# The first loads of q and k cut at another head, fewer filler matmuls, and the last token tile finished in two column halves

## The chip, the cores and the metric

The kernel runs on one core of a Trainium2 chip. The core has five instruction streams: TensorE (PE, matrix products; PEld is its weight load), VectorE (DVE), ScalarE (ACT), GpSimd (POOL) and SyncE (SP, which here only starts transfers). Each stream runs its instructions in program order and waits on semaphores for what the others and the DMA transfers deliver. The metric is the device time of one execution in microseconds (us); lower is better.

## The reference, cut to what matters

Three stages follow one another, all in fp32, on 2 x 576 = 1152 tokens and 512 features (8 heads of 64):

```python
# 1 attention with a causal window of 128 and a bias by distance
scores = q @ k.T / 8;  scores = where(mask, scores - slope_h * |rel|, -1e9)
x = softmax(scores) @ v                       # (B=2, H=8, S=576, D=64) -> (1152, 512)
# 2 dense mixture of 4 experts, F = 1024
p = probs / probs.sum(-1);  x = sum_e p[:, e] * (relu(x @ w1[e]) @ w2[e])
# 3 squared-relu MLP, F = 2048
h = relu(x @ w_in);  out = (h * h) @ w_out
```

## The kernel before

**The work.** fp32 products are made from two rounded parts of each operand (names ending in h and l), so a product is three matmuls. The exception is the very start, where the first 128 tokens of both batch rows are taken in plain fp32 ("raw"): q and k as they were loaded, without a split. The attention is cut into units. A unit of the start covers one pair of heads, 2c and 2c+1 (c = 0 to 3), of both batch rows b, over the first 128 tokens; the text calls these units c0 to c3. For each, `scores` (L802) does four matmuls, g = 0 to 3, with batch row g // 2 and head 2c + g % 2; `top` (L821) reads them on DVE (bias, row minimum); `exp` (L834) runs on ACT; `inv` and `norm` (L842, L850) divide; `turn` (L864) transposes on PE; `hi` (L881) copies; `pv` (L713) multiplies by v. Score tiles have two PSUM buffers (`sc=2`), so the scores of c2 wait until DVE has read those of c0.

**What sets the order.** The class `Plan` (L37) orders the start and the attention at build time: every task has estimated durations on the engines that may run it, dependencies, buffers and a due time, and the planner emits instructions in the order of its own estimated clock. On the chip each engine then follows this fixed order. Where the planner expects PE to stand idle before a task that calls `keep_busy` (L519), it emits small bf16 matmuls of a zero tile (`idle`, 128x128) into the PSUM tile that the task will overwrite; the text calls them fillers. Their number is (expected gap + lead) / each. `plan.at["PE"]` has already been moved past the task when `keep_busy` reads it, so the branch `early` never applies before: lead is -0.2 and each is 0.08 everywhere.

**The first loads.** `first_load` (L1406) brings the first 128 columns of q and k for all 8 heads, 1 MB in all: eight transfers of four heads and one batch row, 128 KB each, into 64 partitions, 512 B per row. Half 0 (heads 0 to 3) serves c0 and c1, half 1 (heads 4 to 7) serves c2 and c3. k of half 0 is started by ACT, the rest by SP, then v and the first weights by SP. In the planner's estimate, c0 and c1 depend on the two tasks of half 0.

```python
src[b, 4 * half:4 * half + 4, 0:D, 0:P]               # L1414, one transfer
lhsT=first_in["q", c // 2][0:D, g // 2, 2 * (c % 2) + g % 2, :]   # L809
```

**The end.** The MLP's last quarters of F run in pairs of token chunks (`gemm1_pair` L1052, `gemm2_pair` L1136). `flush_one` (L1274) does the second product for quarter f of a chunk: for the last chunk (5 token tiles of 128) the quarters f = 2 and f = 3 are summed in one PSUM bank per tile, six matmuls of 512 columns per tile and quarter. After quarter 3 `evac` (L1182) adds the bank to the running sum `ytile` on DVE and SP starts the store to DRAM (L1207). Tile 7 (the fourth of the five) crosses two segments of tokens and is stored by two transfers of 64 rows; tile 8, the last, by one of 128 rows.

Of the kernel before, what the change touches and what calls it, by code (L numbers as in the profile page):

```python
# [8 lines left out]
F32 = mybir.dt.float32  # L9
# [4 lines left out]
ALU = mybir.AluOpType  # L14
PSUM = bass.MemoryType.PSUM

P = 128
# [8 lines left out]
PAIRS = [(0, 256), (512, 320)]  # L26
# [104 lines left out]
def kernel(  # L131
# [14 lines left out]
    nc = tc.nc  # L146
    B, H, _, S = qT.shape
    D = v.shape[2] // H
    NT, DM = out.shape
    E, _, F = w1.shape  # L150
# [5 lines left out]
    NQ = 4  # L156
# [26 lines left out]
    NE = len(w1s)  # L183
# [22 lines left out]
    def w_tile(shape, dtype, name):  # L206
        i = free.pop(0)
        return wbuf[i].tile(shape, dtype, tag=f"wb{i}", name=name), i
# [110 lines left out]
    def spent(eng, us, lag=0.0):  # L319
        clock[eng] = max(clock[eng], clock["now"] + lag) + us  # L320
        return clock[eng]
# [133 lines left out]
    def overlap(a0, an, b0, bn):  # L455
        a, b = max(a0, b0), min(a0 + an, b0 + bn)
        return (a, b - a) if a < b else None

    def tile_runs(nt):

        col = 0
        for s0, sn in SEGS:
            hit = overlap(col, sn, nt * P, P)
            if hit:
                yield hit[0] - nt * P, s0 + hit[0] - col, hit[1]
            col += sn

    def chunks(e):
        return CHUNKS if e else CHUNKS0
# [5 lines left out]
    plan = Plan(SLOTS)  # L475
# [4 lines left out]
        sc=[actx.enter_context(tc.tile_pool(name="psc", bufs=2, space=PSUM))],  # L480
# [4 lines left out]
    def ps_tile(kind, shape, name):  # L485
        pool = psum[kind][0]
        psum[kind].append(psum[kind].pop(0))
        return pool.tile(shape, F32, tag=kind, name=name)
# [30 lines left out]
    def keep_busy(place):  # L519


        early = plan.at["PE"] < 1.0 and plan.gap > 2.0
        lead, each = (0.6, 0.11) if early else (-0.2, 0.08)
        for _ in range(int(max(plan.gap + lead, 0.0) / each)):
            nc.tensor.matmul(  # L525
                out=place, lhsT=idle, rhs=idle, start=True, stop=True, skip_group_check=True
            )
# [45 lines left out]
    def tile_n(t):  # L573
        return min(P, S - t * P)
# [209 lines left out]
    def job_tasks(u, i, t, add, b_, end, ready, G, q0, k0, pos, wide):  # L784
        c = units[u]["c"]
        n = tile_n(t)
# [4 lines left out]
        s = {k: Buf(k) for k in ("sc", "ts", "st", "tp")}  # L791
        cols = [(0, n)] if t == 0 else [(0, P), (P, n)]
        rows = [cn for _, cn in cols]
        key = "j%d" % i
        last = state.get("last", {})
# [6 lines left out]
        def scores(eng):  # L802
            sc = s["sc"].tile = ps_tile("sc", [P, G, w], "sc")
            keep_busy(sc[:, 0, 0:P])
            qs = slice(t * P - q0, t * P - q0 + n)
            for g in range(G):
                if raw:
                    nc.tensor.matmul(
                        out=sc[0:n, g, :], lhsT=first_in["q", c // 2][0:D, g // 2, 2 * (c % 2) + g % 2, :],  # L809
                        rhs=first_in["k", c // 2][0:D, g // 2, 2 * (c % 2) + g % 2, :],  # L810
                        start=True, stop=True,
                    )
                    continue
                for ql in (b_["qh"].tile, b_["ql"].tile):
                    nc.tensor.matmul(  # L815
                        out=sc[0:n, g, :], lhsT=ql[:, g, qs],
                        rhs=b_["khl"].tile[:, g, j0:j0 + w],
                        start=(ql is b_["qh"].tile), stop=(ql is b_["ql"].tile),
                    )
# [120 lines left out]
    ytile = {}  # L940
# [192 lines left out]
        fill(0.6, step, 0.8 + 1.4 * (2 * n // P))  # L1133
        return h

    def gemm2_pair(e, ch, g, h, tile_, first, last):  # L1136
        (wh, _), (wl, _) = w2t[e, g]
        i, y = tile_
        ns = slice(i * P, (i + 1) * P)
        for fo, (hh, hl) in enumerate(h):  # L1140
            for j, (l_, r_) in enumerate(((hh, wh), (hh, wl), (hl, wh))):
                nc.tensor.matmul(  # L1142
                    out=y, lhsT=l_[:, ns], rhs=r_[:, fo, :],
                    start=(first and fo == 0 and j == 0),
                    stop=(last and fo == FTQ - 1 and j == 2),
                )
# [35 lines left out]
    def evac(e, ch, tiles, f=0, two=False):  # L1182
        c0 = PAIRS[ch][0] if two else chunks(e)[ch][0]
        for i, y in tiles:
            nt = c0 // P + i
            if e == 0 or (e == E and f < FT // 2):
                pool = yp if nt < 4 else late["w"]
                ytile[nt] = pool.tile([P, DM], F32, tag=f"y{nt}", name="y")
            yt = ytile[nt]
            spent("ACT" if e == E and f < FT // 2 else "DVE", 0.74, 1.38 if two else 0.69)  # L1190
            if e == 0:
                nc.vector.tensor_scalar(
                    out=yt, in0=y, scalar1=pt[:, nt, 0:1], scalar2=None, op0=ALU.mult
                )
            elif e < E:
                nc.vector.scalar_tensor_tensor(
                    out=yt, in0=y, scalar=pt[:, nt, e:e + 1], in1=yt, op0=ALU.mult, op1=ALU.add
                )
            elif e == E and f < FT // 2:
                nc.scalar.activation(out=yt, in_=y, func=ACTF.Copy)  # L1200
            elif e == E:
                nc.vector.tensor_tensor(out=yt, in0=y, in1=yt, op=ALU.add)
            else:
                nc.vector.tensor_tensor(out=yt, in0=y, in1=yt, op=ALU.add)
            if e == NE - 1 and f == NQ - 1:
                for r0, n0, n in tile_runs(nt):
                    nc.sync.dma_start(out=out[n0:n0 + n, :], in_=yt[r0:r0 + n, :])  # L1207

    def to_x2(nt, kind):
        tp = ps_tile(kind, [P, KT, P], "xtp")  # L1210
        for k in range(KT):
            nc.tensor.transpose(  # L1212
                out=tp[:, k, :], in_=ytile[nt][:, k * P:(k + 1) * P], identity=ident
            )
        ns = slice(nt * P, (nt + 1) * P)
        spent("ACT", 0.6)
        spent("DVE", 0.7)
        nc.scalar.activation(out=xh[:, :, ns], in_=tp, func=ACTF.Copy)
        nc.vector.tensor_tensor(out=xl[:, :, ns], in0=tp, in1=f32(xh[:, :, ns]), op=ALU.subtract)
# [46 lines left out]
    ys = {}  # L1266
# [7 lines left out]
    def flush_one():  # L1274
        e, ch, f, h, two = pend.pop(0)
        if two:
            first, last = f % 2 == 0, f % 2 == 1
        else:
            n = FT // 2 if e == E else FT
            first, last = f % n == 0, f % n == n - 1  # L1280
        if first:
            n = 2 * PAIRS[ch][1] if two else chunks(e)[ch][1]
            ys[e, ch] = [(i, ps_tile("y", [P, DM], "yacc")) for i in range(n // P)]
        for tile_ in ys[e, ch]:
            if two:
                gemm2_pair(e, ch, f, h, tile_, first, last)
            else:
                gemm2(e, ch, f, h, [tile_], first, last)
            if last:
                evac(e, ch, [tile_], f, two)  # L1290
            elif two:
                run_x2("work")
            i = len(ys[e, ch]) - 1 - tile_[0]
            need = 0.8 + (1.38 - 0.74 * last) * i if two else 3.0 + 0.69 * i
            fill(0.5 if two and last else 1.0, 1.38 if two else 0.69, need)
        w_done(w2t, e, ch, f, two)
        if last:
            tiles = ys.pop((e, ch))
            if e == E - 1 and f == NQ - 1:
                x2todo.extend(PAIRS[ch][0] // P + i for i, _ in tiles)  # L1300
# [96 lines left out]
    for c in range(NP):  # L1397
        for own in (True, False):
            task["bias", c, own] = plan.add(
                "bias", [("DVE", 0.45, 0.5), ("ACT", 0.5, 0.6)],  # L1400
                lambda eng, c=c, own=own: build_bias(c, own, eng), deps=[t_rel],
                due=(8.0 if own else 20.0) + c,
            )
    first_in, first_buf, first_x, first_h = {}, [], [], {}

    def first_load(what, half):  # L1406
        t, buf = w_tile([P, 2, 4, P], F32, "first")
        first_buf.append(buf)
        first_in[what, half] = t
        src = qT if what == "q" else kT  # L1410
        queue = nc.scalar if (what, half) == ("k", 0) else nc.sync
        for b in range(B):
            queue.dma_start(
                out=t[0:D, b], in_=src[b, 4 * half:4 * half + 4, 0:D, 0:P].rearrange("a p s -> p a s")  # L1414
            )

    def first_v():
# [5 lines left out]
    for half in range(2):  # L1423
        for i, what in enumerate("qk"):
            task["first", what, half] = plan.add(
                "first" + what, [("ACT" if (what, half) == ("k", 0) else "SP", 1.3, 5.2 if half else 4.2)],
                lambda eng, what=what, half=half: first_load(what, half), due=half + 0.1 * i,
# [235 lines left out]
    for i in range(PER):  # L1663
        weight_load(i)
    t_pt = plan.add("pt", [("SP", 0.6, 6.0)], lambda eng: nc.sync.dma_start(
        out=pt, in_=probs.rearrange("(t p) e -> p t e", p=P)
# [41 lines left out]
    for it, (e, ch, f, two) in list(enumerate(items))[N1:]:  # L1708
# [4 lines left out]
        g = f if two else f // FTQ  # L1713
# [6 lines left out]
        if two:  # L1720
# [4 lines left out]
            h = gemm1_pair(e, ch, f)  # L1725
        else:
# [4 lines left out]
            h = gemm1(e, ch, f)  # L1731
# [22 lines left out]
        last = not two and (e, ch, f) in ((0, len(CHUNKS0) - 1, FT - 1), (E, len(CHUNKS) - 1, FT - 1))  # L1754
# [37 lines left out]
```

## Time and profile before

| | us |
|---|---|
| median of 3 runs | 665.21 (665.19 to 665.52) |
| profiled execution | 664.39 |
| its span (first to last instruction) | 662.6 |
| PE busy | 654.7 |
| DVE, POOL, ACT busy | 471.2, 386.3, 315.2 |

The profiled execution's own time is 1.8 us longer than its span. Engine columns count execution of instructions, not waits; L numbers are lines of the kernel above. "PE busy" is by modelled ends of pipelined matmuls, and the fillers count as busy, too.

### The profile page before, as it was taken

The numbers are of one execution on the slowest core, as the hardware profiler recorded it, in microseconds if no ns is written. First come the engines' busy times: TensorE is split into PE (matmuls) and PEld (weight loads), VectorE is DVE, ScalarE is ACT, GpSimd is POOL, SyncE is SP. The second block draws the span as 40 slices with busy tenths as digits, with TensorE's granted clock in tenths as the row PEclk, the third lists the DMA queues.
The fourth block names the chain that finished last, engine by engine and source line by source line (L and its number), as shares of the span: only waits on it lengthen the run. The fifth ranks groups of instructions, "written<-read, shape, count | busy, mean of one in ns | idle before, by whom it ended". The sixth has DMA issues, their size and how long they took to land.

```text
span 662.6 us, 10910 instructions
## 1 busy us (share of the span) xinstructions
PE 654.7 (99%) x3899; PEld 587.7 (89%) x3899; DVE 471.2 (71%) x989; ACT 315.2 (48%) x763; POOL 386.3 (58%) x457
## 2 busy tenths in 40 slices
PE   9999999999999999999999999999999999999997
PEld 8879988889898898989999899898999999898996
DVE  6998987748888777877876876776578654545453
ACT  6998877624444344343443434333465534334120
POOL 1799966528776653654565454421568984856331
PEclk9999999999999999999999999999999999999999
DMA  9952221021404334344244344344122001100012
GB/s 237 270 144 77 72 77 42 11 65 60 162 33 136 110 124 154 114 128 158 81 144 143 110 145 143 128 161 157 54 91 80 1 14 50 65 1 1 0 65 79
DMA packets 44022, 64.42 MB, mean 97 GB/s; under 512 B 4160, under 2 KB 26176, under 8 KB 43968
## 3 DMA queue, kind: packets, MB, share of 16 engines
q1 hardware_dynamic: 32704, 39.35, 19.3%
q10 hardware_dynamic: 11264, 24.38, 11.7%
q8 instruction: 30, 0.49, 0.3%
q14 instruction: 24, 0.20, 0.1%
HBM read 52.97 MB, written 10.75 MB: 96 GB/s over the span
## 4 chain that ended last, share of the span: by engine, by line
PE 91%; DVE 3%; ACT 2%; POOL 2%; issue 1%; DMA 1%; POOLq 0%; ACTq 0%
PE yacc L1142 30%; PE hps L1064 27%; PE hps L950 13%; PE yacc L1177 13%; PE xps L735 2%; PE tp L871 2%; PE sc L815 2%; PE hps L1589 1%; ACT ts L837 1%; PE sc L525 1%; POOL ts L859 1%; PE xtp L1212 1%; DVE fxwork L986 1%; DMA rk<-in_kT_dram 1%; POOL ql L501 0%
## 5 line engine op out<-in xcount | busy, mean ns | idle before, releaser
L1142 PE MATMUL yacc<-wh,hmem 128*128 128x512 f32 x576 | 183.7, 390 | 0.0
L501 POOL TENSOR_TENSOR wl<-wraw,wh 128x256 fp32r<-128x256 f32 (+1 forms) x107 | 102.9, 986 | 64.3 <-ACT wh L434 51.4
L1142 PEld LDWEIGHTS yacc<-wh,hmem 128*128 128x128 f32 x576 | 108.2, 188 | 21.8
L1142 PE MATMUL yacc<-wl,hmem 128*128 128x512 f32 x288 | 112.4, 390 | 0.0
L1177 PE MATMUL yacc<-wh,hmem 128*128 128x512 f32 x272 | 89.4, 393 | 0.0
L501 POOL TENSOR_TENSOR ls<-wsum,hs 128x256 fp32r<-128x256 f32 x64 | 54.5, 878 | 48.0 <-ACT hs L381 47.5
L1075 ACT ACTIVATE p<-hps 128x256 f32<-128x256 f32 (+1 forms) x64 | 26.3, 410 | 97.8 <-PE hps L1064 97.2
L950 PE MATMUL hps<-xh,wh 128*128 128x384 f32 (+1 forms) x208 | 66.6, 320 | 0.0
L950 PE MATMUL hps<-xh,wl 128*128 128x384 f32 (+1 forms) x208 | 65.5, 315 | 0.0
L950 PE MATMUL hps<-xl,wh 128*128 128x384 f32 (+1 forms) x208 | 65.4, 315 | 0.0
L1079 DVE TENSOR_TENSOR u<-hps,p 128x256 f32<-128x256 f32 (+1 forms) x64 | 29.1, 455 | 50.0 <-PE hps L1064 49.8
L1142 PEld LDWEIGHTS yacc<-wl,hmem 128*128 128x128 f32 x288 | 54.1, 188 | 10.1
L1177 PEld LDWEIGHTS yacc<-wh,hmem 128*128 128x128 f32 x272 | 51.1, 188 | 10.1
L292 DVE SCALAR_TENSOR_TENSOR wconv<-wraw,wconv 128x512 int32<-128x512 int32 x64 | 57.3, 895 | 1.3
L1099 ACT ACTIVATE hmem<-c 128x256 fp32r<-128x256 f32 (+1 forms) x72 | 31.0, 445 | 54.1 <-DVE c L1079 52.8
L501 POOL TENSOR_TENSOR la<-wraw,ha 128x256 fp32r<-128x256 f32 x48 | 44.5, 950 | 20.4 <-ACT ha L367 20.4
L1177 PE MATMUL yacc<-wl,hmem 128*128 128x512 f32 x136 | 53.2, 391 | 0.0
L501 POOL TENSOR_TENSOR hmem<-c,hmem 128x256 fp32r<-128x256 f32 (+1 forms) x32 | 26.9, 859 | 38.3 <-ACT hmem L1095 38.3
L501 POOL TENSOR_TENSOR hmem<-r,hmem 128x384 fp32r<-128x384 f32 x24 | 26.2, 1092 | 39.1 <-ACT hmem L1164 39.1
L1100 DVE SCALAR_TENSOR_TENSOR hmem<-c,hmem 128x256 fp32r<-128x256 f32 (+1 forms) x72 | 38.5, 555 | 14.6 <-ACT hmem L1099 13.3
L837 ACT ACTIVATE ts<-ts,st 128x256 f32<-128x256 f32 (+2 forms) x80 | 37.1, 466 | 7.1 <-DVE st L828 7.0
L950 PEld LDWEIGHTS hps<-xh,wh 128*128 128x128 f32 x208 | 39.2, 189 | 0.7
(142 smaller groups left out, 1738.2 us busy)
## 6 DMA issues: line engine op xcount, KB each, us to landing
wraw<-in_w_dram SPq DMA_DIRECT2D x32, 512.0 KB, 4.1
wraw<-in_w_out_dram ACTq DMA_DIRECT2D x16, 512.0 KB, 3.9
w<-wconv ACTq DMA_DIRECT2D x32, 256.0 KB, 3.9
wraw<-w SPq DMA_DIRECT2D x16, 512.0 KB, 3.7
wraw<-in_w_in_dram ACTq DMA_DIRECT2D x14, 512.0 KB, 3.7
rq<-in_qT_dram SPq DMA_DIRECT2D x8, 256.0 KB, 7.2
out_dram<-y SPq DMA_DIRECT2D x8, 256.0 KB, 2.1
rk<-in_kT_dram SPq DMA_DIRECT2D x8, 192.0 KB, 5.7
```

Source lines behind the costliest of these rows:

```text
L292: nc.vector.scalar_tensor_tensor(out=ai, in0=raw[j][:, :, part], scalar=amount, in1=ai, op0=op, op1=ALU.bitwise_or,)
L501: e.tensor_tensor(out=out, in0=in0, in1=f32(in1), op=ALU.subtract)
L735: nc.tensor.matmul(out=xps[:, :, o0:o0 + w], lhsT=l_, rhs=r_, start=(i == 0 and l_ is wh_ and r_ is hi), stop=(i == len(mm) - 1 and l_ is ...
L837: nc.scalar.activation(out=ts[0:n, g, :], in_=ts[0:n, g, :], func=ACTF.Exp, bias=st[0:n, 0, g:g + 1], scale=-1.0, accum_out=st[0:n, 1, g:g ...
L950: nc.tensor.matmul(out=ps, lhsT=l_[:, k, cs], rhs=r_[:, k, cols], start=(k == 0 and r_ is xh and l_ is wh and not second), stop=(k == KT - ...
L1064: nc.tensor.matmul(out=ps, lhsT=a[l_][:, k, :], rhs=b[r_][:, k, :], start=start and k == 0 and l_ == r_, stop=stop and k == 1 and l_ == 1, ...
L1075: nc.scalar.activation(out=out, in_=x, func=ACTF.Copy)
L1079: nc.vector.tensor_tensor(out=out, in0=x, in1=y, op=ALU.add)
L1099: nc.scalar.activation(out=hh, in_=src, func=ACTF.Relu)
L1100: nc.vector.scalar_tensor_tensor(out=hl, in0=src, scalar=0.0, in1=f32(hh), op0=ALU.max, op1=ALU.subtract)
L1142: nc.tensor.matmul(out=y, lhsT=l_[:, ns], rhs=r_[:, fo, :], start=(first and fo == 0 and j == 0), stop=(last and fo == FTQ - 1 and j == 2),)
L1177: nc.tensor.matmul(out=y, lhsT=l_[:, ns], rhs=r_[:, fo, :], start=(first and j == 0), stop=(last and j == 2),)
```

## The change

Three edits. `first_load` now cuts after head 1: for each of q, k and each batch row there is one transfer of heads 0 and 1 (64 KB) and one of heads 2 to 7 (192 KB); ACT starts three of them (both small ones of k, then the large one of k for b = 0), SP the other five. The planner's tasks and their estimates stay as they are. `keep_busy` subtracts 1.4 or 1.2 us in place of 0.2 from the expected gap, early in the plan. And the last token tile of the last chunk takes a new function `close`: its quarter 2 gets a bank of its own, which DVE adds to `ytile` at once, and its quarter 3 is made in two halves of 256 columns, each in its own bank, with its own add and its own store, the first half's store from SP, the second half's from ACT.

```diff
@@ keep_busy
-        early = plan.at["PE"] < 1.0 and plan.gap > 2.0
-        lead, each = (0.6, 0.11) if early else (-0.2, 0.08)
-        for _ in range(int(max(plan.gap + lead, 0.0) / each)):
+        lead = -1.4 if plan.at["PE"] < 6.0 else -1.2 if plan.at["PE"] < 9.0 else -0.2
+        for _ in range(int(max(plan.gap + lead, 0.0) / 0.08)):
@@ scores
-                        out=sc[0:n, g, :], lhsT=first_in["q", c // 2][0:D, g // 2, 2 * (c % 2) + g % 2, :],
-                        rhs=first_in["k", c // 2][0:D, g // 2, 2 * (c % 2) + g % 2, :],
+                        out=sc[0:n, g, :], lhsT=first_in["q", g // 2][0:D, 2 * c + g % 2, :],
+                        rhs=first_in["k", g // 2][0:D, 2 * c + g % 2, :],
@@ gemm2_pair
-                    out=y, lhsT=l_[:, ns], rhs=r_[:, fo, :],
+                    out=y, lhsT=l_[:, ns], rhs=r_[:, fo, cols],
@@ new
+    def close(e, ch, f, h, i):
+        nt = PAIRS[ch][0] // P + i
+        if f < NQ - 1:
+            y = ps_tile("y", [P, DM], "yacc")
+            gemm2_pair(e, ch, f, h, (i, y), True, True)
+            nc.vector.tensor_tensor(out=ytile[nt], in0=y, in1=ytile[nt], op=ALU.add)
+            return
+        for cs, queue in ((slice(0, DM // 2), nc.sync), (slice(DM // 2, DM), nc.scalar)):
+            y = ps_tile("work", [P, DM // 2], "ylast")
+            gemm2_pair(e, ch, f, h, (i, y), True, True, cs)
+            yt = ytile[nt][:, cs]
+            nc.vector.tensor_tensor(out=yt, in0=y, in1=yt, op=ALU.add)
+            for r0, n0, n in tile_runs(nt):
+                queue.dma_start(out=out[n0:n0 + n, cs], in_=yt[r0:r0 + n, :])
@@ flush_one
         for tile_ in ys[e, ch]:
+            if (e, ch) == (NE - 1, len(PAIRS) - 1) and f >= NQ - 2 and tile_ is ys[e, ch][-1]:
+                close(e, ch, f, h, tile_[0])
+                break
@@ first_load
-        for b in range(B):
+        some, most = slice(0, 2), slice(2, H)
+        for b, heads in {
+            ("q", 0): ((0, some), (1, some)), ("k", 0): ((0, some), (1, some), (0, most)),
+            ("q", 1): ((0, most), (1, most)), ("k", 1): ((1, most),),
+        }[what, half]:
+            queue = nc.scalar if (what, half) == ("k", 0) else nc.sync
             queue.dma_start(
-                out=t[0:D, b], in_=src[b, 4 * half:4 * half + 4, 0:D, 0:P].rearrange("a p s -> p a s")
+                out=first_in[what, b][0:D, heads, :],
+                in_=(qT if what == "q" else kT)[b, heads, 0:D, 0:P].rearrange("a p s -> p a s"),
```

By this the fillers before the scores of c0 fall from 51 to 36, those before the scores of c2 from 17 to 5; the later groups (20, 1 and 6) stay. No other instruction of the start changes its place in its stream.

PE at the start, before: the scores of c0 (tile sc_158) and of c1 (sc_214), after the 51 fillers. The DMAHW names are the semaphores of the eight first transfers.

```order
L808 MATMUL sc_158<-first_127,first_124 128x128 [waits DMAHW1_49,DMAHW0_49]
L808 MATMUL sc_158<-first_127,first_124 128x128
L808 MATMUL sc_158<-first_127,first_124 128x128 [waits DMAHW3_49,DMAHW2_49]
L808 MATMUL sc_158<-first_127,first_124 128x128
L808 MATMUL sc_214<-first_127,first_124 128x128 x4
```

The same place now, after 36 fillers: c0 is sc_158, c1 is sc_199.

```order
L807 MATMUL sc_158<-first_128,first_124 128x128 [waits DMAHW1_49,DMAHW0_49]
L807 MATMUL sc_158<-first_128,first_124 128x128
L807 MATMUL sc_158<-first_129,first_125 128x128 [waits DMAHW3_49,DMAHW2_49]
L807 MATMUL sc_158<-first_129,first_125 128x128
L807 MATMUL sc_199<-first_128,first_124 128x128 [waits DMAHW5_49,DMAHW4_49]
L807 MATMUL sc_199<-first_128,first_124 128x128
L807 MATMUL sc_199<-first_129,first_125 128x128 [waits DMAHW7_49,DMAHW6_49]
L807 MATMUL sc_199<-first_129,first_125 128x128
```

Before, c1 waits for no transfer that c0 has not waited for. Now c1 waits for the other four of the eight first transfers.

SP's first transfers before: q of half 0, q of half 1, k of half 1, then v and the first weights.

```order
L1413 DMA first_124<-in_qT_dram 64x4x128 x2
L1413 DMA first_130<-in_qT_dram 64x4x128 x2
L1413 DMA first_147<-in_kT_dram 64x4x128 x2
L1421 DMA first_156<-in_v_dram 128x2x512
L215 DMA wraw_224<-in_w1_dram 128x4x256
```

SP's first transfers now: heads 0 and 1 of q for both batch rows, heads 2 to 7 of q, heads 2 to 7 of k for b = 1, then v and the first weights.

```order
L1440 DMA first_124<-in_qT_dram 64x2x128
L1440 DMA first_125<-in_qT_dram 64x2x128
L1440 DMA first_124<-in_qT_dram 64x6x128
L1440 DMA first_125<-in_qT_dram 64x6x128
L1440 DMA first_129<-in_kT_dram 64x6x128
L1449 DMA first_156<-in_v_dram 128x2x512
L215 DMA wraw_209<-in_w1_dram 128x4x256
```

SP has one transfer fewer ahead of v (five, six before); ACT has one more ahead of its first computation (three, two before).

DVE at the very end, before: the five adds of the last chunk, tile 4 to tile 8 (y_5929).

```order
L1204 TENSOR_TENSOR y_5751<-yacc_7145,y_5751 128x512
L1204 TENSOR_TENSOR y_5759<-yacc_7146,y_5759 128x512
L1204 TENSOR_TENSOR y_5906<-yacc_7147,y_5906 128x512
L1204 TENSOR_TENSOR y_5915<-yacc_7148,y_5915 128x512
L1204 TENSOR_TENSOR y_5929<-yacc_7149,y_5929 128x512
```

The same place now; tile 8 is y_5902, its quarter 2 comes first.

```order
L1214 TENSOR_TENSOR y_5902<-yacc_7146,y_5902 128x512
L1203 TENSOR_TENSOR y_5724<-yacc_7118,y_5724 128x512
L1203 TENSOR_TENSOR y_5732<-yacc_7119,y_5732 128x512
L1203 TENSOR_TENSOR y_5879<-yacc_7120,y_5879 128x512
L1203 TENSOR_TENSOR y_5888<-yacc_7121,y_5888 128x512
L1220 TENSOR_TENSOR y_5902<-ylast_7187,y_5902 128x256
L1220 TENSOR_TENSOR y_5902<-ylast_7196,y_5902 128x256
```

DVE has one add of 512 columns more, and two of 256 columns in place of the last one. On PE, twelve matmuls of 256 columns end the program where six of 512 did.

## Rows read from the trace of the kernel before

**Rows 1.** The page: the chain that ended last, share of each engine.
```profile
PE 91%; DVE 3%; ACT 2%; POOL 2%; issue 1%; DMA 1%; POOLq 0%; ACTq 0%
```

**Rows 2.** Stretches: length, PE, PEld, DVE, ACT, POOL busy, granted clock, DMA share, GB/s.
```profile
0.00:20.00 20.00, 18.56 (x187) 16.25 (x187) 13.94 (x68) 14.70 (x53) 4.67 (x11) 1.00 0.97 237
40.00:50.00 10.00, 9.09 (x52) 6.61 (x51) 8.74 (x24) 9.26 (x27) 10.00 (x9) 1.00 0.54 149
```

**Rows 3.** Timeline of the start: start, length, engine, line, operation, count, idle before.
```profile
0.98 4.70 PE L525 MATMUL sc<-idle 128*128 128x128 bf16 x51 [0.98 <-DVE idle L1389]
0.98 3.92 PE L525 MATMUL sc<-idle 128*128 128x128 bf16 x37 [0.98 <-DVE idle L1389]
6.96 0.29 DVE L828 CUSTOM_DVE_ANT_0 ts<-sc,bias 128x128 f32<-128x128 f32 x1 [3.27 <-PE sc L808]
7.94 1.11 PE L525 MATMUL sc<-idle 128*128 128x128 bf16 x17
7.96 0.29 DVE L828 CUSTOM_DVE_ANT_0 ts<-sc,bias 128x128 f32<-128x128 f32 x1
9.38 0.69 DVE L853 TENSOR_TENSOR ts<-ts,st 128x512 f32<-128x512 f32 x1
10.18 0.29 DVE L828 CUSTOM_DVE_ANT_0 ts<-sc,bias 128x128 f32<-128x128 f32 x1
14.94 0.69 DVE L853 TENSOR_TENSOR ts<-ts,st 128x512 f32<-128x512 f32 x1
```

**Rows 4.** The chain that ended last, at the start: start, length, what.
```profile
5.68 1.25 PE sc L808 x8
9.05 1.10 PE sc L808 x8
10.51 3.20 ACT ts L837 x16
```

**Rows 5.** Timeline: issues of the second q transfer and the last k transfer.
```profile
1.56 0.83 SPq L1413 DMA_DIRECT2D first<-in_qT_dram  x1
4.46 0.62 SPq L1413 DMA_DIRECT2D first<-in_kT_dram  x1
```

**Rows 6.** Landing after issue (us, last number): first k, second q, last k transfer.
```profile
first<-in_kT_dram ACTq DMA_DIRECT2D x1, 128.0 KB, 3.0
first<-in_qT_dram SPq DMA_DIRECT2D x1, 128.0 KB, 4.5
first<-in_kT_dram SPq DMA_DIRECT2D x1, 128.0 KB, 4.5
```

**Rows 7.** Stretches (columns as rows 2): first loads on two queues, then on SP's alone.
```profile
3.00:4.50 1.50, 1.50 (x17) 1.50 (x16) 0.68 (x6) 1.49 (x7) 0.00 (x0) 1.00 0.97 211
4.75:7.25 2.50, 2.50 (x30) 2.31 (x28) 0.29 (x3) 0.01 (x1) 0.00 (x0) 1.00 1.23 183
```

**Rows 8.** Timeline of the end: last add, last two issues of stores.
```profile
658.50 0.69 DVE L1204 TENSOR_TENSOR y<-yacc,y 128x512 f32<-128x512 f32 x1 [0.67 <-PE yacc L1142]
658.42 0.59 SPq L1207 DMA_DIRECT2D out_dram<-y  x1
659.22 0.42 SPq L1207 DMA_DIRECT2D out_dram<-y  x1
```

**Rows 9.** The end: two stretches of the stores, and the last store's landing.
```profile
659.60:659.80 0.20, 0.00 (x0) 0.00 (x0) 0.00 (x0) 0.00 (x0) 0.00 (x0) 1.00 0.83 205
660.40:660.60 0.20, 0.00 (x0) 0.00 (x0) 0.00 (x0) 0.00 (x0) 0.00 (x0) 1.00 1.03 389
out_dram<-y SPq DMA_DIRECT2D x1, 256.0 KB, 2.3
```

**Rows 10.** Matmuls of 256 columns in a row; DVE adds of 256 columns (mean ns).
```profile
30.46 0.28 PE L950 MATMUL hps<-xl,wh 128*128 128x256 f32 x1
30.58 0.28 PE L950 MATMUL hps<-xh,wl 128*128 128x256 f32 x1
L1079 DVE TENSOR_TENSOR u<-hps,p 128x256 f32<-128x256 f32 x1 | 0.4, 425 | 1.7 <-PE hps L1064 1.7
```

More of the change, by code (lines that the diff above doesn't have):

```diff
@@ L1134, in gemm1_pair, with gemm2_pair @@
         return h
-    def gemm2_pair(e, ch, g, h, tile_, first, last):
+    def gemm2_pair(e, ch, g, h, tile_, first, last, cols=slice(0, DM)):
         (wh, _), (wl, _) = w2t[e, g]
@@ L1282, in flush_one @@
             n = 2 * PAIRS[ch][1] if two else chunks(e)[ch][1]
-            ys[e, ch] = [(i, ps_tile("y", [P, DM], "yacc")) for i in range(n // P)]
+            ending = (e, ch, f) == (NE - 1, len(PAIRS) - 1, NQ - 2)
+            ys[e, ch] = [
+                (i, None if ending and i == n // P - 1 else ps_tile("y", [P, DM], "yacc"))
+                for i in range(n // P)
+            ]
         for tile_ in ys[e, ch]:
+            if (e, ch) == (NE - 1, len(PAIRS) - 1) and f >= NQ - 2 and tile_ is ys[e, ch][-1]:
+                close(e, ch, f, h, tile_[0])
+                break
             if two:
@@ L1406, in first_load @@
     def first_load(what, half):
[L1407 to L1411, printed above, removed]
-        for b in range(B):
+        if half == 0:
+            for b in range(B):
+                t, buf = w_tile([P, H, P], F32, "first")
+                first_buf.append(buf)
+                first_in[what, b] = t
+        some, most = slice(0, 2), slice(2, H)
[4 more added lines that the diff above has]
+            queue = nc.scalar if (what, half) == ("k", 0) else nc.sync
             queue.dma_start(
-                out=t[0:D, b], in_=src[b, 4 * half:4 * half + 4, 0:D, 0:P].rearrange("a p s -> p a s")
+                out=first_in[what, b][0:D, heads, :],
+                in_=(qT if what == "q" else kT)[b, heads, 0:D, 0:P].rearrange("a p s -> p a s"),
             )
```

## The prediction, written before the changed kernel was run

> **What bounds the kernel now.** I read the page first, then stretches of time, then the timeline and the landing of single transfers in the two places that the change touches. The page's chain is PE for 91% [rows 1], so anything that holds PE back early is paid at the end unless a later wait swallows it. The stretches say how much could be swallowed: PE stands idle for 1.44 us of the first 20, and for 0.91 us between 40 and 50, where POOL is busy 10.00 of 10 [rows 2].
>
> The start is a relay of three engines. PE runs 51 fillers for 4.70 us, then the scores of c0 from 5.68 to 6.93; DVE waits 3.27 us and starts on them at 6.96; it starts on c1 at 7.96, normalizes c0 at 9.38 and c3 at 14.94 [rows 3, 4]. Between 6.96 and 15.6 DVE hardly stops: its one visible pause is between 10.07 (9.38 + 0.69) and 10.18, where it waits for the scores of c2, which ended at 10.15 (9.05 + 1.10) behind 17 fillers [rows 3, 4]. ACT runs its exponentials just as tightly, the last 16 records end at 13.71 [rows 4]. So in this stage the DVE stream decides: it may start c1 at most 0.1 us later than now before the end of the stage moves.
>
> The end is one tile: the last add takes 0.69 us from 658.50, the store is issued at 659.22 and lands 2.3 us later [rows 8, 9].
>
> **The change part by part.** *Fillers and the scores of c0.* 15 of 51 fillers go. They are not all of one price: the first 37 took 3.92 us, 0.106 each, the other 14 the remaining 0.78 us, 0.056 each [rows 3]. The 15 come off the fast end: 15 x 0.056 = 0.84 us. c0's scores would start at 5.68 - 0.84 = 4.84 and, at the 1.10 us of an undisturbed group [rows 4], end at 5.94 instead of 6.93. Their data: the second q transfer was issued at 1.56 and landed 4.5 later, at 6.06, inside c0's scores [rows 5, 6]; it now carries half the bytes and has half as many ahead, so I expect it near 5.0. c0 gains 1.0 us.
>
> *The scores of c1.* This is the step that decides. By the order, c1 now waits for all eight first transfers, the last being heads 2 to 7 of k for b = 1, the fifth on SP. Before it needed only the first four (landed by 6.06), and the complete megabyte only at c2. When is the megabyte complete? Now: issue 4.46 plus 4.5 = 8.96 [rows 5, 6]. The change moves the same bytes into the same 64 partitions. With only SP's queue left the engines were 1.23 busy at 183 GB/s, so an earlier issue (five instead of six on SP, about 0.7 us) buys nothing where the engines are the limit [rows 7]. Bound below: if all of it ran at the rate with two queues, 211 GB/s [rows 7], 1049 KB would take 4.97 instead of 5.73 us, 0.76 less: 8.2. Bound above: the four small transfers put 256 KB less into the queues at first; 128 KB at 183 GB/s is 0.7 us: 9.7. I take 9.0, next to the row. The last two of c1's four matmuls come after it, half of 1.10: c1 ends at 9.55 (8.75 to 10.25). DVE would begin on it there instead of at 7.96: 1.6 us later, less the 0.1 pause, 1.5 (0.7 to 2.2).
>
> Behind the wait: PE's stream is in order, so c2's five fillers and c2, c3 and the transposes stand behind c1. On DVE, the normalizing of c0 stands behind c1's reduction, and so c0's head start of 1.0 us ends as idle time of DVE. ACT finishes c0's exponentials early and waits. Taking 12 fillers from in front of c2 (12 x 0.065 = 0.8 us by the 17 in 1.11 [rows 3]) is worth the 0.1 us pause at most, and nothing once DVE is late. The third issue on ACT, 0.62 to 0.83 us by SP's [rows 5], delays its table load and bias tiles, hidden by the exponentials' start near 6.2.
>
> *How much of it stays.* All three engines are delayed together, and what they feed (first 16 us) is a stream with PE idle only 1.44 us in 20 [rows 2]. The idle 0.91 us at 40 to 50 stands beside a full POOL, whose operands are delayed, too. I keep 0.95 of it: 1.4 us. If those 0.91 us were true slack, 0.6 would stay.
>
> *The end.* PE: twelve matmuls of 256 columns, 0.12 apart [rows 10], 1.44 us, for six of 512; the last PE instruction ends within 0.1 us of now. The last add shrinks from 0.69 to 0.43 [rows 8, 10]: the second half's store can be issued some 0.2 us earlier, and on ACT's queue. The first half's add is done by 658.3, but SP is issuing tile 7's second store until 659.01 (658.42 + 0.59) [rows 8], so it starts no sooner than the second half's. And the engines are full there: 0.83 busy at 205 GB/s on tile 7's 64-row stores, then 1.03 busy at 389 GB/s on tile 8's [rows 9]. The bytes must pass in any case. I take -0.1: -0.4 if the halves slip in beside tile 7's slow stores, +0.2 if 1 KB rows move worse than 2 KB rows. The extra add (0.69) of quarter 2 falls into 0.67 us pauses and before them: nothing.
>
> The Trainium skill speaks against this part: "DMA: Bandwidth & Descriptors", section "Issuing engines are not separate DMA queues", says that transfers started by SP and ACT run on the same engines and interleave, and that starting from both saves only issue time. By it the end would be worth 0, by the earlier add alone -0.2.
>
> Sum: +1.4 - 0.1 = +1.3. Against the profiled execution that is 664.39 + 1.3 = 665.7; that execution (span 662.6 plus 1.8) was 0.8 under the median, so against the median: 665.21 + 1.3 = 666.5.
>
> **The rivals.** *The large transfers land in time.* Two queues stay busy longer (ACT carries 320 KB instead of 256), and if the megabyte is in by 7.6, c1 ends by 8.1 and costs nothing; my bound of 8.2 falls 0.6 short of that, and the 1.23 busy share is against it. Then c2's fillers give 0.1 back and the end 0.2: 664.9, not slower. It decides from a landing of 7.5 on.
>
> *The delay is swallowed.* POOL at 10.00 of 10 may be paced by transfers that do not move; then 0.6 of delay less 0.1: 665.7. For it: the one large PE pause lies there. Against: POOL's operands come from the delayed engines.
>
> *The clock falls.* PE would stand still from about 6 to 9 us except for two matmuls. The trace of before has no pause over 1 us and a granted clock of 1.00, the 2.4 GHz level, in every stretch of [rows 2, 7], though its first fillers ran at half pace. If the pace of the first fillers returned (0.106 for 0.056), the rest of c1 costs 0.55 more, c2 and c3 1.1 each, of which DVE's own work hides some 0.5: 2.2 us more, 668.7. The Trainium skill's "TensorE: Matmul & The Clock Gate", section "Why this matters for your kernels", warns of pauses between bursts of matmuls for this reason; no row here shows a pause as long.
>
> **How the numbers follow.** Forecast 0.55, in time 0.12, swallowed 0.18, clock 0.15. Of 8 in 10: from the in-time case, 664.7, to near the clock case, 668.5. The forecast alone spans 665.5 (0.7 of delay - 0.4) to 667.5 (2.1 + 0.2). 0.2% is 1.33 us, about what a measurement of this kernel tells from no change: slower means over 666.54. Half of the forecast and the clock case lie above: 0.28 + 0.15 = 0.43; faster, under 663.88, needs a landing before 7.5 and a better end at once: 0.05; the rest 0.52.
>
> **What would show it.** In the changed trace: c0's scores from about 4.8; c1's first two matmuls near 7 and its last two after 9, PE idle between; DVE's first c1 row near 9.6 with a wait on PE of over 2 us ahead of it; the normalizing of c3 ending near 17.1 instead of 15.6; the later stages shifted by the same 1.4 us; the last add 0.43 us long, the last landing within 0.3 us of now, counted from PE's end. Wrong would be: DVE on c1 before 8.1, or a shift that is gone by 50 us.

## The result: 4.3 us slower, and the profile after

The changed kernel took 669.65 us (median of 4, 669.38 to 670.2) against 665.37 us beside it (median of 4, 665.19 to 665.84): ratio 1.0064, 95% interval 1.0047 to 1.0082. The forecast was 666.5 with a range up to 668.5: the sign was in the forecast, the size was outside the range. The execution with a profile took 669.38 us, its span is 667.6 (before: 664.39 and 662.6).

First the stretches (columns as in [rows 2]); the last line is the second of them in the trace of the kernel before.

```profile
6.00:7.00 1.00, 0.18 (x2) 0.00 (x0) 0.78 (x7) 0.45 (x3) 0.00 (x0) 1.00 1.14 180
8.00:9.00 1.00, 0.00 (x0) 0.00 (x0) 0.00 (x0) 0.20 (x2) 0.00 (x0) 0.78 1.05 219
9.00:10.00 1.00, 0.39 (x2) 0.42 (x3) 0.00 (x0) 0.00 (x0) 0.00 (x0) 0.50 1.02 356
10.00:18.00 8.00, 8.00 (x48) 7.29 (x48) 5.43 (x32) 4.95 (x24) 0.00 (x0) 0.50 1.10 302
18.00:19.00 1.00, 1.00 (x12) 0.73 (x9) 0.93 (x4) 0.00 (x0) 0.00 (x0) 0.60 1.25 216
```
```profile
8.00:9.00 1.00, 1.00 (x18) 0.90 (x17) 0.92 (x9) 1.00 (x7) 0.00 (x0) 1.00 1.00 264
```

Two things are new. Between 8 and 9 us PE and DVE stand still and ACT nearly so, where before PE and ACT were busy without a break (1.00) and DVE for 0.92. And the granted clock, 1.00 in all of [rows 2], is 0.50 (the 1.2 GHz level) from inside the stretch 8 to 9 until 18 to 19. PE then counts as busy 8.00 of 8, but with only 48 matmuls in it: busy at half pace.

PE's timeline says what it waited for (start, length, engine, line, operation, count, idle before and its releaser).

```profile
0.99 4.02 PE L524 MATMUL sc<-idle 128*128 128x128 bf16 x36 [0.99 <-DVE idle L1411]
4.94 1.24 PE L807 MATMUL sc<-first 64*128 64x128 f32 x8
7.20 0.68 PE L807 MATMUL sc<-first 64*128 64x128 f32 x4 [1.01 <-DMA first<-in_qT_dram]
9.61 1.19 PE L807 MATMUL sc<-first 64*128 64x128 f32 x4 [1.74 <-DMA first<-in_kT_dram]
11.38 3.78 PE L807 MATMUL sc<-first 64*128 64x128 f32 x16
16.00 2.34 PE L524 MATMUL xps<-idle 128*128 128x128 bf16 x20
18.27 0.89 PE L719 MATMUL xps<-pt,first 128*64 128x128 f32 x8
```

The scores of c0 do begin earlier (4.94; before 5.68, [rows 4]). The 36 fillers took 4.02 us, 0.11 each: in the kernel before, the 37 fillers at this pace were followed by 14 at twice the pace [rows 3], and here those are gone. The scores of c1 come in two halves, each behind a large transfer. The second half, four records, lasts 1.19 us where the first half lasted 0.68, and c2 and c3 together (16 records) last 3.78, where a group of eight took 1.10 to 1.25 before [rows 4].

The transfer that ended the second wait: its issue, and its landing after issue.

```profile
3.80 0.64 SPq L1440 DMA_DIRECT2D first<-in_kT_dram  x1
```
```profile
first<-in_kT_dram SPq DMA_DIRECT2D x1, 192.0 KB, 5.7
```

So it landed at 9.5 us; before, the last k transfer landed at 8.96 [rows 5, 6]. DVE's timeline carries the delay on:

```profile
6.22 0.29 DVE L827 CUSTOM_DVE_ANT_0 ts<-sc,bias 128x128 f32<-128x128 f32 x1 [2.52 <-PE sc L807]
10.95 0.29 DVE L827 CUSTOM_DVE_ANT_0 ts<-sc,bias 128x128 f32<-128x128 f32 x1 [3.80 <-PE sc L807]
13.49 0.29 DVE L827 CUSTOM_DVE_ANT_0 ts<-sc,bias 128x128 f32<-128x128 f32 x1 [0.60 <-PE sc L807]
15.20 0.29 DVE L827 CUSTOM_DVE_ANT_0 ts<-sc,bias 128x128 f32<-128x128 f32 x1 [0.78 <-PE sc L807]
19.27 0.69 DVE L852 TENSOR_TENSOR ts<-ts,st 128x512 f32<-128x512 f32 x1
```

DVE begins c1 at 10.95 (7.96 before, [rows 3]), waits 0.60 and 0.78 us more for the slow scores of c2 and c3, and ends the normalizing of c3 at 19.27 + 0.69 = 19.96 instead of 15.63 [rows 3]: 4.33 us late, which is the whole loss of 4.28. Followed back, the chain that ended last now runs, behind SP's issues, through this transfer (start, length, what), where it had the fillers and scores of c0 before [rows 3, 4]:

```profile
3.80 5.67 DMA first<-in_kT_dram
```

The end, for comparison with [rows 8, 9] (timeline, then the landing of the last two stores):

```profile
663.04 0.28 PE L1141 MATMUL ylast<-wh,hmem 128*128 128x256 f32 x1
663.36 0.42 DVE L1220 TENSOR_TENSOR y<-ylast,y 128x256 f32<-128x256 f32 x1 [0.29 <-PE ylast L1141]
663.81 0.37 ACTq L1222 DMA_DIRECT2D out_dram<-y  x1
663.90 0.54 SPq L1222 DMA_DIRECT2D out_dram<-y  x1
```
```profile
out_dram<-y SPq DMA_DIRECT2D x3, 128.0 KB, 2.7
```

The add is 0.42 instead of 0.69, but the first half's store waits for SP's queue until 663.90 and lands 2.7 later (the median of three like it), at about 666.6. From the start of the last add that is 3.2 us; before it was 659.22 + 2.3 - 658.50 = 3.0 [rows 8, 9].

### The profile page after: what moved, and what is told of

Read it like the earlier page. It is cut to its first block, busy times and chain, and to the rows that moved or that the text cites. A ratio compares the mean times of both kernels' runs of the same rounds, so it can differ in the third digit from the quotient of the medians.

```text
span 667.6 us, 10873 instructions
## 1 busy us (share of the span) xinstructions
PE 657.9 (99%) x3878; PEld 590.4 (88%) x3878; DVE 469.9 (70%) x991; ACT 315.2 (47%) x763; POOL 387.1 (58%) x457
## 4 chain that ended last, share of the span: by engine, by line
PE 94%; POOL 2%; DMA 1%; DVE 1%; issue 1%; ACT 1%; SPq 0%; POOLq 0%
PE yacc L1141 29%; PE hps L1063 26%; PE hps L949 14%; PE yacc L1176 14%; PE xps L734 3%; PE tp L870 2%; PE sc L814 2%; PE hps L1617 1%; DMA first<-in_kT_dram 1%; PE sc L807 1%; PE xtp L1227 1%; DVE fxwork L985 1%; POOL ts L858 1%; POOL ql L501 0%; SPq L1440 0%
```

## The experiments

Two causes stood side by side in one trace: the wait for the transfers (theory 1, first half) and the granted clock (second half). The first four runs separate them and the three parts of the change.

**The changed kernel with PE kept at work in the wait** (*hold_clock*).

```
+ if c == 1 and g in (0, 2):
+     for _ in range(18 if g == 0 else 31):  # a filler into sc[:, 3, 0:P]
```

> The changed kernel with 49 more filler matmuls inside the scores of c1 (18 ahead of its first matmul, 31 between its second and third), so that PE has work while it waits for the transfers; nothing else differs. Theory 1 (two causes: c1 waits for the last of the large transfers, and the granted clock falls to 0.50 during that wait and makes everything to about 19 us run at half pace): the wait stays (last k transfer near 9.5 us, c1 ends near 10.2), the granted clock stays at 1.00 through the first 20 us, the scores of c2 and c3 take about 2.1 instead of 3.78 us, the 20 fillers about 1.1 instead of 2.34, and the time falls by about 3 us, to 666.6 (666.0 to 667.3). Rival A (the wait alone costs the 4 to 5 us, the half pace lies beside it): clock at 1.00 but time within 0.7 us of the changed kernel's 669.65. Rival B (the pauses have nothing to do with the clock): granted clock falls to 0.50 all the same and the time stays 669.65.

Measured: 667.48 us (666.94 to 667.82), ratio to before 1.0033 (1.0021 to 1.0045). PE's timeline, and the stretch in which the clock had been low:

```profile
7.26 0.68 PE L813 MATMUL sc<-first 64*128 64x128 f32 x4 [0.52 <-DMA first<-in_qT_dram]
9.71 0.71 PE L813 MATMUL sc<-first 64*128 64x128 f32 x4
10.74 2.05 PE L813 MATMUL sc<-first 64*128 64x128 f32 x16
```
```profile
10.00:18.00 8.00, 7.31 (x80) 6.11 (x79) 7.16 (x38) 6.49 (x28) 0.40 (x1) 1.00 1.10 307
```

The issue of the last k transfer and its landing after issue, then DVE's first row of c1 and the normalizing of c3:

```profile
3.81 0.63 SPq L1446 DMA_DIRECT2D first<-in_kT_dram  x1
```
```profile
first<-in_kT_dram SPq DMA_DIRECT2D x1, 192.0 KB, 5.6
```
```profile
10.57 0.29 DVE L833 CUSTOM_DVE_ANT_0 ts<-sc,bias 128x128 f32<-128x128 f32 x1 [3.96 <-PE sc L813]
17.14 0.69 DVE L858 TENSOR_TENSOR ts<-ts,st 128x512 f32<-128x512 f32 x1
```

The transfer lands at 9.4 (3.81 + 5.6), near the 9.5 of the changed kernel, and c1's second half still comes behind it; the clock is 1.00, c2 and c3 take 2.05 instead of 3.78, and the normalizing of c3 ends at 17.14 + 0.69 = 17.83. The difference between the two kernels with the same transfers is 669.65 - 667.48 = 2.2 us: the clock. What is left over the kernel before, 667.48 - 665.26 = 2.2 us, is the wait, together with what the 49 added fillers cost: the last 31 run to 9.79 us (7.88 + 1.91), past the landing. Theory 1 holds in kind, but the time lies just above its range and the clock share is smaller than the 3 us I had expected; rivals A and B fall.

**The cut of the transfers alone** (*loads_only*): the new first transfers and scores; fillers and end as before.

> The kernel before with the new cut of the first transfers and the scores that go with it; fillers (51 and 17) and the end are as before. Theory 1: the cut alone makes c1 wait for the last large transfer (near 9.5 us) and PE's pause during it (about 7.9 to 9.6) brings the clock down, so that nearly the whole loss is there: 668 to 670 us. Rival (the clock falls because the fillers were taken away): the wait stays, but the granted clock is 1.00 through the start, and the time is 666.3 to 667.5, that is 2 us over the kernel before and no more.

Measured: 669.5 us, 1.0063 (1.0046 to 1.008). Nearly the whole loss is in the cut. Five of six executions, with a mean granted clock of 0.991 to 0.994, took 669.14 to 670.9; the sixth, at 0.999, took 666.74, which is 1.5 over the kernel before: a wait without the fall, though a single execution without a trace. In the trace the second half of c1 runs at full pace, DVE begins c1 at 10.01, and the clock falls after that:

```profile
9.19 0.68 PE L808 MATMUL sc<-first 64*128 64x128 f32 x4 [1.43 <-DMA first<-in_kT_dram]
10.85 3.65 PE L808 MATMUL sc<-first 64*128 64x128 f32 x16
```
```profile
10.01 0.29 DVE L828 CUSTOM_DVE_ANT_0 ts<-sc,bias 128x128 f32<-128x128 f32 x1 [2.43 <-PE sc L808]
```
```profile
11.00:12.00 1.00, 1.00 (x6) 1.00 (x7) 0.89 (x3) 0.99 (x6) 0.00 (x0) 0.51 1.10 354
```

**The fillers alone** (*fillers_only*): 36 and 5 instead of 51 and 17; transfers and end as before.

> The kernel before with only the number of fillers changed (36 instead of 51 ahead of c0, fewer ahead of c2 and c3); transfers and end as before. Theory 1: c0's scores still wait for the second q transfer, which landed at 6.06 us, and c2's for the last k transfer at 8.96; the pauses are short, the clock stays at 1.00, and the time stays at 665.0 to 665.6. Rival (fewer fillers are enough to bring the granted clock down): granted clock 0.50 somewhere between 6 and 16 us and 667 us or more.

Measured: 666.62 us (666.31 to 667.99), 1.0024 (1.0013 to 1.0034). Theory 1 was wrong here and its rival right about the clock, though not about the time (667 or more): there is no pause over 0.23 us in front of the scores, and still the clock falls, at 9.1 us in the trace. Five of the seven executions, at a mean granted clock of 0.994 or 0.995, took 666.31 to 666.74; the two at 0.999 and 1.000 were longer, 667.77 and 667.99, and stay unexplained.

```profile
4.94 1.06 PE L807 MATMUL sc<-first 64*128 64x128 f32 x4
6.22 1.57 PE L807 MATMUL sc<-first 64*128 64x128 f32 x12 [0.23 <-DMA first<-in_qT_dram]
9.31 2.90 PE L807 MATMUL sc<-first 64*128 64x128 f32 x12 [0.20 <-DMA first<-in_kT_dram]
```
```profile
9.00:10.00 1.00, 0.80 (x4) 0.72 (x4) 0.93 (x3) 1.00 (x7) 0.00 (x0) 0.55 1.04 369
```

Either part brings the clock down by itself, so their costs don't add: 1.4 + 4.2 would be 5.6, the whole change cost 4.3.

**The end alone** (*tail_only*).

> The kernel before with only the end of the change: the last token tile's last quarter in two column halves with two banks and two queues. Theory 1 (the bytes of tiles 7 and 8 fill the transfer engines whoever issues them): 665.2 to 665.6, no difference. Rival A (the earlier, narrower last add is worth its 0.2 to 0.4 us): 664.8 to 665.1. Rival B (1 KB rows move worse than 2 KB rows): 665.7 to 666.0.

Measured: 665.65 us (664.74 to 666.2) beside 665.26; ratio 1.0004 (0.9995 to 1.0012): no difference clear of the noise. The time lies between the ranges of theory 1 and rival B; rival A's gain is excluded beyond 0.3 us, rival B's loss is not (the interval reaches 0.8 us).

Next: which fillers hold the clock, whether c1's wait goes away with another cut, and whether PE or DVE carries the half pace to the end.

**51 and 5 fillers, 36 and 17 fillers** (*fill_c2*, *fill_c0*; the kernel before otherwise).

```
- lead, each = (0.6, 0.11) if early else (-0.2, 0.08)
+ lead = -1.2 if 6.0 <= plan.at["PE"] < 9.0 else -0.2    # fill_c2
+ lead = -1.4 if plan.at["PE"] < 6.0 else -0.2           # fill_c0
```

> The kernel before with 5 instead of 17 fillers ahead of c2, the 51 ahead of c0 kept; nothing else. Theory 2 (the fillers ahead of c2 hold the clock, since they stand in the one stretch between 7.9 and 9.0 us where PE has little else): the granted clock falls to 0.50 near 9.5 us as it did with both groups cut, time 666.3 to 666.9. Rival (the fillers ahead of c0 hold it): clock 1.00 throughout and 665.0 to 665.6.

> The kernel before with 36 instead of 51 fillers ahead of c0, the 17 ahead of c2 kept; nothing else. Theory 2 (the fillers ahead of c2 hold the clock): granted clock 1.00 throughout, 665.0 to 665.6. Rival (the fillers ahead of c0 hold it): clock 0.50 from near 9.5 us, 666.3 to 666.9.

Measured: *fill_c2* 664.38 us (664.06 to 664.99), 0.9992 (0.9984 to 1.0001), granted clock 0.997 or more in all 11 executions. *fill_c0* 667.54 us (663.95 to 669.5), 1.0026 (1.001 to 1.0043), in two groups: six executions at a mean granted clock of 0.992 to 0.994 took 667.22 to 668.42, five at 0.998 to 1.000 took 663.95 to 665.06. (The twelfth, 669.5 at 1.000, stays unexplained.) Theory 2 fell: with all fillers ahead of c0 the clock holds, without 15 of them it falls in half of the executions; those ahead of c2 only cost time (*fill_c2* came out 0.6 us under its rival's range). The same kernel with and without the fall differs by some 3.4 us. In the profiled execution of *fill_c0*:

```profile
6.33 1.57 PE L807 MATMUL sc<-first 64*128 64x128 f32 x12 [0.88 <-DMA first<-in_qT_dram]
9.94 3.78 PE L807 MATMUL sc<-first 64*128 64x128 f32 x16
```
```profile
5.00:6.00 1.00, 0.46 (x4) 0.27 (x3) 0.00 (x0) 0.00 (x0) 0.00 (x0) 1.00 1.16 184
8.00:9.00 1.00, 0.96 (x10) 0.96 (x10) 0.93 (x8) 1.00 (x7) 0.00 (x0) 0.50 0.95 330
```

The fillers end before q of b = 1 has landed, PE waits 0.88 us, and at 8 us the clock is 0.50. In *fill_c2*, where the fillers reach up to c0, c2 is scored at 8.19 without loss:

```profile
5.20 2.37 PE L807 MATMUL sc<-first 64*128 64x128 f32 x16
8.19 2.18 PE L807 MATMUL sc<-first 64*128 64x128 f32 x16
```

**The changed kernel without the 20 fillers ahead of c0's product with v** (*no20*).

```
- keep_busy(xps[:, 0:P])
+ if c:
+     keep_busy(xps[:, 0:P])
```

> The changed kernel without the 20 fillers ahead of c0's product with v; nothing else. Theory 1 (part of what the half clock costs is that these fillers last 2.34 us instead of about 1.1 and so outlast the copy of the probabilities they were to bridge, which ends near 17.0 us): that product begins about 1.2 us earlier, near 17.1 instead of 18.34, and the time is 668.3 to 669.1. Rival A (DVE's stream of normalizings decides, not PE): 669.4 to 669.9. Rival B (without them the low clock lasts longer): granted clock 0.50 beyond 20 us and 670 or more.

Measured: 669.94 us (669.51 to 671.26), 0.3 over the changed kernel, whose own executions spread over 0.8: no gain. The product begins at 17.16, 1.1 us earlier, as theory 1 said, and DVE gains nothing by it: the normalizing of c3 ends at 20.14, 0.18 later, as the second half of c1's scores began 0.18 later (9.79 against 9.61). That is rival A's reason. Rival B is half right: the low clock lasts longer, still 0.77 on average between 20 and 22. What that costs behind the start, and whether it hides a gain of PE, this run does not separate:

```profile
17.16 1.12 PE L720 MATMUL xps<-pt,first 128*64 128x128 f32 x8 [0.78 <-DVE pt L497]
```
```profile
20.00:22.00 2.00, 2.00 (x18) 1.50 (x17) 1.42 (x3) 1.89 (x4) 1.62 (x2) 0.77 0.04 10
```

**A cut into three** (*thirds*): heads 0 and 1, 2 and 3, 4 to 7.

> The kernel before with a third cut of the first transfers: heads 0 and 1, then heads 2 and 3, then heads 4 to 7, each for q and k and both b (twelve transfers; k's first four on ACT, the rest on SP); fillers (51 and 17) and the end as before. Theory 1 (c1 waited only because its heads came inside the large transfers): c0 and c1 are scored without a pause between them, DVE begins c1 by 8.0 us, c2's data land 0.3 to 0.8 us later than before's 8.96 because SP issues two more transfers, the granted clock holds, and the time is 665.3 to 666.0. Rival A (more and smaller transfers move worse: c1 waits all the same): DVE on c1 after 8.5, 666.5 or more. Rival B (the later data of c2 give PE a pause that brings the granted clock to 0.50): 666.6 to 667.6.

Measured: 665.96 us (664.74 to 670.77) beside 664.89, 1.0025 (1.001 to 1.004). c1 no longer waits, one group of sixteen scores from 6.33 to 8.38; two executions of eleven, at 0.997 and 0.996, took 668.94 and 670.77.

```profile
6.33 2.05 PE L808 MATMUL sc<-first 64*128 64x128 f32 x16
```

So the wait of c1 belongs to the large transfers, not to cutting as such; but the third cut gains nothing either, it costs 0.1 to 0.4% by the interval. In this execution the 51 fillers lasted until c0 could only begin at 6.33, DVE began c0 at 7.53 and c1 at 8.53, later than the 8.0 expected, though c1 did not wait.

**Towards a better version** (*even51*, *even44*: three cuts, q on SP and k on ACT; *fill_move*: 36 fillers ahead of c0, 15 inside its wait, 5 ahead of c2; *fill_c2* once more).

> A version meant to beat both: first transfers as heads 0 and 1, then 2 and 3, then 4 to 7, q's six on SP and k's six on ACT, 51 fillers ahead of c0 and 5 ahead of c2, end as before. Theory 3 (the start is bound by when the last transfer lands and by the end of the fillers; both queues issuing brings the last landing from 8.96 to about 8.2): c1 without a wait, c2 scored from about 8.3, DVE's normalizing of c3 ends near 15.0, clock 1.00, 664.2 to 664.8. Rival A (ACT's bias tiles, 1.3 us later behind four more issues, hold up the exponentials): 665.2 or more, DVE waiting for ACT in the start. Rival B (the start's length does not reach the end): 664.9 to 665.4.

> The same with 44 instead of 51 fillers ahead of c0. Theory 3: c0's scores begin 0.4 to 0.7 us earlier, DVE on c0 near 6.2, 663.8 to 664.6 in the executions in which the clock holds. Rival (fillers ahead of c0 hold the clock, so with fewer of them it falls in part of the executions): single times of 667 to 669 with a granted clock of 0.99 among them.

> The kernel before with 36 fillers ahead of c0, 15 more between the second and third matmul of c0 (where it waits for q of b = 1, near 5.5 to 6.1 us) and 5 ahead of c2. Theory 4 (not the number ahead of c0 counts but that PE is at work without a stop until 6 us): no execution with the granted clock below 0.997, 664.2 to 664.9, as with 51 ahead of c0 and 5 ahead of c2. Rival (it is the number ahead of c0): part of the executions at a clock of 0.99 and 667 to 668.

> The kernel before with 5 instead of 17 fillers ahead of c2, once more, beside the other versions on one chip. Expected again 0.0 to 0.7 us under the kernel before, clock 1.00 throughout; if the small lead was chance: 665.0 to 665.5.

Measured beside 665.15 us: *even51* 665.59, 1.0016 (1.0004 to 1.0028); *even44* 665.7, 1.0012 (1.0003 to 1.0021); *fill_move* 664.81, 0.9993 (0.9984 to 1.0002); *fill_c2* again 664.69, 0.999 (0.9982 to 0.9999). Theory 3 fell: in *even51* the last q transfer, on SP, ended a wait of 1.97 us of c2 and the clock was 0.50 from 11 us on; single executions reached 668.81. So 51 fillers ahead of c0 do not hold the clock against a later wait. In *even44* four of eleven executions, at 0.995, took 666.87 to 667.32.

```profile
10.55 2.71 PE L807 MATMUL sc<-first 64*128 64x128 f32 x12 [1.97 <-DMA first<-in_qT_dram]
```

Theory 4 held: with the 15 fillers moved into the wait the clock was 0.999 or more in all 11 executions. (The number of fillers ahead of c1 is the same 51, so work in the wait and their sum are not told apart.) *fill_c2*, the only version measured twice, was about 0.5 us, 0.1%, below the kernel before both times, though the interval of the first just includes no change: the one part of the change that may be useful is the smaller number of fillers ahead of c2.

## Why the prediction was wrong

Each kernel's profiled execution: when the normalizing of c3 ended on DVE (start in the timeline + 0.69), and the time of that execution.

| kernel | c3 normalized, us | its own time, us |
|---|---|---|
| before | 15.63 | 664.39 |
| fill_c2 | 15.14 | 664.38 |
| even44 | 15.56 | 665.54 |
| tail_only | 15.64 | 664.74 |
| fill_c2_again | 16.17 | 664.95 |
| thirds | 16.20 | 664.74 |
| fill_move | 16.20 | 665.07 |
| fillers_only | 17.00 | 666.74 |
| hold_clock | 17.83 | 667.52 |
| even51 | 18.06 | 667.45 |
| fill_c0 | 18.52 | 668.06 |
| loads_only | 19.29 | 669.14 |
| after | 19.96 | 669.38 |
| no20 | 20.14 | 670.12 |

- *The step that failed: the clock.* I had it as a rival at 0.15, with a price of 2.2 us, and left it out of the sum because the trace of before showed 1.00 everywhere and no pause over 1 us. That was no reason: I had worked out myself that the change makes PE stand still from about 6 to 9 us. It came, and *hold_clock* prices it at 2.2 us. That my price was the same is partly luck, since it is no fixed one: *fillers_only* lost 1.4 us in all with it, and in *fill_c0* executions with and without the fall differ by 3.4. My total for that rival, 668.7, is 0.95 under the result. What I did not see is that the fillers, which I costed only by the 0.84 us they take, are also what keeps the clock up: *fill_c0* takes 15 away and changes nothing else, and the clock fell in half of its executions; *fill_move* puts them into c0's wait, and it held. The trace of before could not show this price; the chance I gave it was the error. The sentence of the Trainium skill that I cited ("TensorE: Matmul & The Clock Gate", section "Why this matters for your kernels"), on pauses between bursts, pointed the right way; *fillers_only* shows that here the clock fell even without a pause over 0.23 us ahead of the scores.
- *The wait of c1: right in kind, too small.* c1 waits for all eight transfers, PE idle in between, as forecast. The last landed at 9.5, not 9.0 (inside my bounds of 8.2 to 9.7). With c1's scores at full pace DVE began c1 at 10.01 in *loads_only*, where I had 9.55: 2.05 late instead of 1.6. *hold_clock* puts the wait at 2.2 us of time, where the sum had 1.4; but DVE began c1 at 10.57 there, so some half a microsecond of it may belong to the added fillers, and the one execution of *loads_only* without the fall lost 1.5. The wait is 1.5 to 2.2 us, then, and the clock has the rest of the 4.3.
- *How much stays.* I kept 0.95 of the delay; all of it stayed, as far as single profiles show. From before to *hold_clock* c3 moved by 2.20 us and the median by 2.2; from there to the changed kernel by 2.13 and 2.2. In the table the time follows from 17 us on; between 15.1 and 16.2 it does not (664.4 to 665.5, in no order), so half a microsecond of delay more than before is not seen in the time. The slack of 0.91 us beside POOL took up nothing: PE's wait for POOL is 0.9 in both traces, and the matmuls behind it begin at 46.58 before and at 51.82 after.
- *c0's start* gained 0.74 us on DVE (6.96 to 6.22; forecast 1.0) and it was idle time, as forecast. *Twelve fillers ahead of c2*: I gave leaving them out 0.1 us at most; *fill_c2* gains about 0.5.
- *The end*: forecast -0.1 (-0.4 to +0.2), measured by the ratio +0.3 (-0.3 to +0.8). By the Trainium skill's rule ("DMA: Bandwidth & Descriptors", section "Issuing engines are not separate DMA queues") it would be 0 or -0.2; the measured interval holds both and does not tell them apart.

## What to carry to other kernels

Before you take filler work away, ask what it does besides filling time: a trace with the granted clock at 1.00 everywhere does not show what holds it there, and the price of losing it (here 1.4 to 3.4 us) belongs into the sum with a chance, not beside it. When a transfer is cut so that its first part comes early, look for the next reader of the rest: here c1 inherited the wait of c2, at a point where DVE had nothing else to do. And when two parts of a change can each bring the same loss, test each part alone; their losses do not add.

## What was not expected of the hardware

- The granted clock fell to 0.50 at 8.6 us in the changed kernel (after PE had been busy 0.18 and 0.68 in the two stretches before), at 9.1 in *fillers_only* (after stretches of 0.87 and 0.93), near 8 in *fill_c0*, near 11 in *loads_only*; it was back at 1.00 by 19, 16, 19 and 18 us. From 10 us on PE counted as busy in nearly all of the low stretch.
- The pace of the first fillers differs between executions at a granted clock of 1.00: 36 took 3.54 to 4.02 us, 51 took 4.28 to 5.62. c0's start in *fill_c2* moved by 1.3 us (5.20 and 6.54) between two profiled executions, their times by 0.57.
- More issues from a second queue did not bring the complete megabyte earlier: its last part ended a wait at 9.61 (three on ACT) and at 10.55 (*even51*, six on ACT), against a landing at 8.96 before.
- Open: single executions were long at a granted clock of 0.999 to 1.000 (669.5 in *fill_c0*, 669.51 in *no20*, 667.77 and 667.99 in *fillers_only*, 667.03 in *even51*). None of them has a trace. The granted clock cannot settle it: the first fillers of the kernel before ran at half pace (0.106 us each) where it reads 1.00 [rows 3, 7].
